# Reordering the end of an attention kernel's load phase: one chunk of q loaded ahead of the last rows of k, k's inverse norms ended on VectorE, and the first tile of v loaded and turned in two halves

## The chip, the cores and the metric

The kernel runs on one core of a Trainium2 chip, as one program. Its time is device time in microseconds (us); the median of the runs is what counts.

The engines are named as in the profile: PE is TensorE (matmuls), PEld its weight loads, DVE is VectorE, ACT is ScalarE, POOL is GpSimd, SP is SyncE. Here POOL issues the loads of q, k, v and the weights, and SP issues the stores and the transposing copies of later v tiles.

## The reference

The arrays q, k and v have the shape (4, 6080, 256) and are float32. For each of the four batches b:

```
qn = q / (norm of q over its 6080 rows + 1e-6)      # one norm per column
kn = k / (norm of k over its 6080 rows + 1e-6)
a  = softmax(kn.T @ qn / tau)                       # 256 x 256, tau = 1
x  = v @ a                                          # 6080 x 256
out = (s * relu(x @ w_in)**2 + b_) @ w_out          # w_in 256 x 2048, w_out 2048 x 256
```

So all of q and k of a batch has to be seen before the first row of its output can be made. After that the work on v is a long stream of matmuls.

## The kernel before

**Stages.** Batch 0's Gram matrix (k.T q, 256 x 256, in `s_ps`) and its column norms are computed first, while q and k arrive. The softmax matrix is never applied to v by itself: `first_block` and `folds` multiply it by w_in, giving `wa` (256 x 2048), and the stream then computes `h = wa.T @ vT` (line 790), relu, square and the second matmul, group after group of 512 rows of v (`mm1`, `relu`, `square`, `plain_mm2`, `seven_items`). The Gram matrices of batches 1 to 3 are interleaved into the stream. The change lies wholly in the stage before the stream and in its first matmuls.

**Chunks.** Batch 0's rows go in 13 chunks: chunks 0 to 10 hold 512 rows (4 rows on each of 128 partitions, `jc` = 4), and chunks 11 and 12 share the last 448 rows (2 rows on each of 112 partitions, `jc` = 2). The last three, 10 to 12, are the `late` ones. For every chunk there are Gram matmuls (`mm`, line 173), squares of k and q (`squares`, lines 198 to 206), and sums of the squares. For the early chunks DVE folds the squares into one tile (`fold`, `into_first`, lines 218 and 232). For the late ones the squares go straight into the norm matmuls: line 271 for k (a row of 256 sums spread over all partitions), line 275 for q (one column of sums for each half); chunk 10's k is first halved by an add (line 248).

**Inverse norms.** `inverse` (line 296) makes 1 / (sqrt(n) + 1e-6) in four ACT steps: Ln, Exp(0.5 x), Ln(x + eps), Exp(-x). k has 256 columns per partition, q two. `scale` (line 321) multiplies `s_ps` by k's inverse norms in two halves into `sm_t`. `exps` (line 327) then applies q's inverse norms as the scale of an Exp and gives `eT`. From `eT` come the row sums (line 367), the first products with w_in (lines 372 and 377), the reciprocal of the sums (line 381) and the scaled `wa` (ACT line 348, DVE line 350).

**Order.** `po` keeps instructions in the order in which the program issues them, so each engine's queue is written by hand. DMA loads all go through POOL's queue in program order; each of them waits for the one eight places ahead of it to have landed. Before the change the end of that queue for batch 0 is: k of chunk 10, k of chunks 11 and 12 (one transfer), q of chunk 10, q of chunk 11, q of chunk 12, v tile 0, then w_in in five pieces (256, 256, 512, 512 and 512 columns).

On the other engines the order before is: all of k's squares (chunk 10 and 11 on ACT, 12 on DVE) and k's norm matmuls, k's four ACT steps, then q's squares on DVE, chunk by chunk with the Gram matmuls of the late chunks, then q's four ACT steps, `scale`, the transposes of v tile 0 on PE with one DVE copy (`transpose_v`, lines 496 and 498), one `keep_busy` matmul (line 583, whose result nothing uses), and `first_block`.

Of the kernel before, what the change touches and what calls it, by code (L numbers as in the profile page):

```python
# [8 lines left out]
FP16 = mybir.dt.float16  # L9
# [7 lines left out]
def kernel(  # L17
# [12 lines left out]
    nc = tc.nc  # L30
    P = 128
# [23 lines left out]
    def po(ins):  # L55

        tc.keep_in_program_order(ins)
        return ins
# [53 lines left out]
    class Gram:  # L112
# [69 lines left out]
        def norm_ops(self, c):  # L182

            qc, kc = self.tiles[c]
            _, np_, jc = self.chunks[c]
            st = {}

            at_end = self.b == 0 and c >= len(self.chunks) - NLATE

            def squares(a, js):  # L190
                def f():
                    if "sq" not in st:
                        if at_end:
                            st["sq"] = late_pool.tile([P, 2, jc, C], FP16, tag=f"sq{c}", name="sq")
                        else:
                            st["sq"] = sq_pool.tile([P, 2, JC, C], FP16, tag="sq", name="sq")
                    if a == 1 and at_end and c == len(self.chunks) - 1:
                        po(nc.vector.tensor_mul(
                            st["sq"][:np_, 1, js, :], kc[:np_, js, :], kc[:np_, js, :]))
                    elif a == 0 and (self.b > 0 or at_end or c % 2 == 0):  # L200
                        po(nc.vector.tensor_mul(  # L201
                            st["sq"][:np_, 0, js, :], qc[:np_, js, :], qc[:np_, js, :]))
                    else:
                        po(nc.scalar.activation(  # L204
                            out=st["sq"][:np_, a, js, :], in_=(qc, kc)[a][:np_, js, :],
                            func=AF.Square))
                return f

            def fold(half, arrays, last):
                def f():  # L210
                    src = st["f", 2 * half] if 2 * half < jc else st["sq"]
                    if ("f", half) not in st:
                        if last:
                            t = f3_pool.tile([P, 2, 1, C], FP16, tag="f3", name="f3")
                        else:
                            t = sq_pool.tile([P, 2, half, C], FP16, tag=f"f{half}", name="f")
                        st["f", half] = t
                    po(nc.vector.tensor_add(  # L218
                        st["f", half][:np_, arrays], src[:np_, arrays, :half, :],
                        src[:np_, arrays, half : 2 * half, :]))  # L220
                    if last and c == 0:
                        self.first = st["f", half]
                    if last and c == 0:
                        for rows in self.rows:
                            rows.append((st["f", half], np_, 1))
                return f

            def into_first():

                dst, src = self.first[:np_], st["f", 1][:np_]  # L230
                if self.b == 0:
                    po(nc.vector.tensor_add(dst, dst, src))  # L232
                else:
                    po(nc.gpsimd.dma_start(out=dst, in_=src, accum_op=ALU.add))  # L234

            def unfolded(a):
                self.rows[a].append((st["sq"], np_, jc))

            ops = []
            for h in range(0, jc, 4):  # L240
                js = slice(h, min(h + 4, jc))
                ops += [squares(1, js), squares(0, js)]
            if at_end:
                def rows(a):
                    if a == 0 or jc == 2:
                        return unfolded(a)
                    half = sq_pool.tile([P, 2, 2, C], FP16, tag="f2", name="half")
                    po(nc.vector.tensor_add(half[:np_, 1], st["sq"][:np_, 1, :2], st["sq"][:np_, 1, 2:]))
                    self.rows[1].append((half, np_, 2))
                return ops + [rows]  # L250
            if jc == 8:
                ops += [fold(4, slice(0, 1), False), fold(4, slice(1, 2), False)]
            ops += [fold(2, slice(0, 2), False), fold(1, slice(0, 2), True)]
            return ops + [into_first] if c > 0 else ops
# [24 lines left out]
        def finish_ops(self):  # L279
# [3 lines left out]
            def inverse(a=None):  # L283

                n = C + CH if a is None else (CH, C)[a]

                def part(i):
                    if i == 0:
                        st["r", a] = sm_pool.tile([P, n], FP32, tag=f"r{a}", name=f"r{a}")
                        if a is None:  # L290
                            st["r", 1], st["r", 0] = st["r", a][:, :C], st["r", a][:, C:]
                    r = st["r", a]
                    func, kw = [(AF.Ln, dict(bias=tiny)), (AF.Exp, dict(scale=0.5)),
                                (AF.Ln, dict(bias=eps)), (AF.Exp, dict(scale=-1.0))][i]
                    sums = self.n_all if a is None else self.n_ps[a]
                    po(nc.scalar.activation(out=r, in_=r if i else sums, func=func, **kw))  # L296
                    if i == 3 and a != 1 and inv_tau != 1.0:
                        po(nc.vector.tensor_scalar_mul(
                            out=st["r", 0], in0=st["r", 0], scalar1=inv_tau))

                return [lambda i=i: part(i) for i in range(4)]
# [57 lines left out]
            def first_block(n):  # L359
# [15 lines left out]
                for m in range(CH):  # L375
                    for j in range(CH):
                        po(nc.tensor.matmul(second[:, m], st["e"][:, j, ts(m, P)],
                                            w_in16[:, j, ds(n, n)], start=(m == 0 and j == 0),
                                            stop=(j == CH - 1), skip_group_check=True))
                st["rs"] = sm_pool.tile([P, CH], FP32, tag="rs", name="rs")  # L380
                po(nc.vector.reciprocal(out=st["rs"], in_=r_ps))
                for f0 in range(0, n, P):
                    for m in range(CH):
                        scaled(f0, P, m, two[m][:, ds(f0, P)])
                for m in range(CH):
                    scaled(n, n, m, second[:, m])

# [88 lines left out]
    def group(g):  # L476
        t0 = g * TG
        return t0, min(TG, NT - t0) // P

    v_tiles, vT_tiles = {}, {}  # L480

    def load_v(g):
        t0, nj = group(g)
        v16 = vpool.tile([P, TG // P, C], FP16, tag="v16", name="v16")
        po(nc.gpsimd.dma_start(  # L485
            out=v16[:, :nj, :],
            in_=v_flat[t0 : t0 + nj * P, :].rearrange("(p j) c -> p j c", j=nj)))
        v_tiles[g] = v16

    def transpose_v(g):  # L490
        _, nj = group(g)
        v16 = v_tiles.pop(g)
        vT_ps = ps_o.tile([P, CH, TG], FP16, tag="o_ps", name="vT_ps")
        for j in range(nj):
            for ch in range(CH):
                po(nc.tensor.transpose(vT_ps[:, ch, ts(j, P)], v16[:, j, ts(ch, P)], ident16))
        vT = vtpool.tile([P, CH, TG], FP16, tag="vT", name="vT")
        po(nc.vector.tensor_copy(out=vT[:, :, : nj * P], in_=vT_ps[:, :, : nj * P]))
        vT_tiles[g] = vT

    def crossbar_v(g):

# [39 lines left out]

    for i in range(2):
        g0.load(len(g0.chunks) - NLATE, (i,))
        g0.load_last(i)
    NW = 512
    w_in_rows = moe_w_in.rearrange("(co p) f -> p co f", p=P)
# [2 lines left out]
        cs = slice(0, CH) if co is None else slice(co, co + 1)  # L550
        po(nc.gpsimd.dma_start(out=w_in16[:, cs, f0:f1], in_=w_in_rows[:, cs, f0:f1]))

    load_v(0)
    load_w_in(0, 2 * P)
    load_w_in(2 * P, NW)
    load_w_in(NW, 2 * NW)
    load_w_in(2 * NW, 3 * NW)
    load_w_in(3 * NW, Dff)
    w_out_rows = moe_w_out.rearrange("(fo p) d -> p fo d", p=P)
# [39 lines left out]

    sum_rows = [rows.pop() for rows in g0.rows]  # L600
    ops = {c: g0.norm_ops(c) for c in late}
    for c in late:
        k_squares, _, into_rows = ops[c]
        k_squares()
        into_rows(1)
        g0.add_norms(1)
    last_sum()
    for rows, row in zip(g0.rows, sum_rows):
        rows.append(row)
    for f in (norms_k, *inverse_k):  # L610
        f()
    for c in late:
        ops[c][1]()
        ops[c][2](0)
        if c == NCH0 - 1:
            norms_q()
        for j in range(g0.chunks[c][2]):
            g0.mm(c, j)
        if c < NCH0 - 1:
            g0.add_norms(0)  # L620
    for f in (*inverse_q, scale_s):
        f()
    transpose_v(0)
    keep_busy(1)
    first_block()

# [146 lines left out]
    def mm1(g, m):  # L773
# [4 lines left out]
        i, fh = divmod(m, 2)  # L778
        if fh == 0:
            h_tiles[g, i] = h_tile("h_ps")  # L780
        h_ps = h_tiles[g, i][:, fh, :]
        for b, p0, p1 in segments(g):
            wa = grams[b].wa
# [274 lines left out]
```

## Time and profile before

| what | value |
|---|---|
| median of 3 runs | 713.63 us (713.52 to 713.67) |
| the profiled execution: its own time | 713.68 us |
| its span in the trace | 712.0 us, so 1.7 us lie around it |
| PE busy in the span | 690.0 us, 97% |
| DVE, ACT, POOL busy | 635.0, 548.2, 109.9 us |
| PE busy from 50 us to the end | 659.09 of 662.00 us |
| PE busy in 24.00 to 31.60, and 31.60 to 38.40 | 4.71 of 7.60, and 6.15 of 6.80 us |

Times in the trace count from the start of the span. A timeline row gives the start, the duration, engine, line, operation, destination and sources, shapes and count. An arrow in brackets is the idle time ahead of the row and what ended it. A row with a count above 1 merges neighbours, and its duration runs from the first start to the last end. An operation's duration holds a fixed part that overlaps with the next operation on the same engine.

### The profile page before, as it was taken

To read this page: it belongs to the slowest core of one execution; us is meant where nothing else is said; L and a number is where in the kernel's file an instruction comes from. 1 tells how busy PE (TensorE), PEld (TensorE's weight loads), DVE (VectorE), ACT (ScalarE), POOL (GpSimd) and SP (SyncE) were. 2 spreads that over 40 slices of the span, in tenths; PEclk is the share of its full clock that TensorE was granted. 3 is DMA by queue.
4 is the path that set the end of the run, shared out by engine and by line. 5 is a ranking of instruction groups with operands and counts; after the bars stand their busy time and mean duration, and the time that the engine had idled before them with its cause. 6 is when DMAs were issued, how large, how long until landed. Compare 5 with 4: busy or idle time off the path is not lost.

```text
span 712.0 us, 17517 instructions
## 1 busy us (share of the span) xinstructions
PE 690.0 (97%) x7422; PEld 501.8 (70%) x7422; DVE 635.0 (89%) x906; ACT 548.2 (77%) x599; POOL 109.9 (15%) x184
## 2 busy tenths in 40 slices
PE   3699999999999999999999999999999999999998
PEld 2456777776677777777677777777768777777777
DVE  3889999999988989998999899998998888888886
ACT  5789877787787777778877777777877777777875
POOL 3433132202102132111010222111000000000000
PEclk9999999999999999999999999999999999999999
DMA  9999999756746889465761888737423333321202
GB/s 240 207 253 158 189 170 132 130 93 123 140 103 107 132 142 152 98 96 102 155 127 50 149 143 143 128 76 100 99 64 74 94 71 76 97 61 46 83 31 75
DMA packets 86846, 83.81 MB, mean 118 GB/s; under 512 B 56240, under 2 KB 62432, under 8 KB 86512
## 3 DMA queue, kind: packets, MB, share of 16 engines
q0 software_dynamic: 26000, 43.74, 38.8%
q1 hardware_dynamic: 60336, 37.71, 22.3%
q8 instruction: 58, 0.95, 0.6%
q10 hardware_dynamic: 432, 1.25, 0.4%
q14 instruction: 20, 0.16, 0.1%
HBM read 78.91 MB, written 24.90 MB: 146 GB/s over the span
## 4 chain that ended last, share of the span: by engine, by line
PE 95%; DVE 2%; DMA 1%; ACT 1%; issue 0%; DVEq 0%
PE h_ps L790 46%; PE o_ps L961 40%; PE s_ps L173 4%; DVE f L218 1%; PE wa_ps L421 1%; DMA raw<-in_q_dram 1%; PE o_ps L865 1%; PE o_ps L837 0%; DVE f L232 0%; ACT r L296 0%; PE wa_ps L355 0%; DVE sq L201 0%; ACT sq L204 0%; ACT qk L164 0%; PE n_ps L271 0%
## 5 line engine op out<-in xcount | busy, mean ns | idle before, releaser
L800 ACT ACTIVATE r<-h_ps 128x1024 f16<-128x1024 f32 (+1 forms) x384 | 388.5, 1013 | 144.5 <-PE h_ps L790 140.9
L790 PE MATMUL h_ps<-vT,wa 128*128 128x512 f16 (+7 forms) x1632 | 451.9, 364 | 0.0
L961 PEld LDWEIGHTS <-S 128*128 128x128 f16 x2944 | 198.1, 98 | 84.3
L961 PEld LDWEIGHTS <-g 128*128 128x128 f16 x2208 | 155.0, 98 | 74.0
L813 DVE TENSOR_TENSOR g<-r 128x2048 f16<-128x2048 f16 (+2 forms) x150 | 174.6, 1164 | 10.0 <-ACT r L800 9.5
L961 PE MATMUL o_ps<-T,S 128*128 128x128 f16 x2208 | 183.1, 219 | 0.0
L790 PEld LDWEIGHTS <-wa 128*128 128x128 f16 x1632 | 136.6, 98 | 18.8 <-ACT wa L348 0.6
L961 PE MATMUL o_ps<-w_out,g 128*128 128x128 f16 x1472 | 134.2, 219 | 0.0
L811 ACT ACTIVATE g<-r 128x1024 f16<-128x1024 f16 (+1 forms) x97 | 100.3, 1034 | 0.2
L818 DVE SCALAR_TENSOR_TENSOR o_sb<-o_ps,s_out,u 128x256 f32<-128x256 f32 x138 | 66.3, 481 | 36.0 <-PE o_ps L961 34.2
L173 PE MATMUL s_ps<-qk 128*128 128x256 f16 (+1 forms) x384 | 68.9, 280 | 16.6 <-ACT qk L164 11.0
L485 POOL DMA_DIRECT2D v<-in_v_dram x48 | 31.4, 662 | 241.0 <-DMA vT<-v 164.5
L234 POOL DMA_DIRECT2D f<-f x33 | 28.9, 875 | 246.9 <-DVE f L218 167.3
L818 DVE SCALAR_TENSOR_TENSOR u<-o_ps,s_out,rowconst 128x256 f32<-128x256 f32 x138 | 65.9, 477 | 0.0
L961 PE MATMUL o_ps<-w_out,S 128*128 128x128 f16 x736 | 63.5, 219 | 0.0
L961 PE MATMUL o_ps<-N,g 128*128 128x128 f16 x736 | 63.4, 219 | 0.0
L890 DVE TENSOR_TENSOR S<-S,g 128x2048 f16<-128x2048 f16 (+1 forms) x47 | 56.4, 1201 | 1.2
L204 ACT ACTIVATE sq<-qk 128x1024 f16<-128x1024 f16 (+2 forms) x53 | 54.5, 1041 | 2.7 <-DVE f L218 2.3
L888 DVE TENSOR_TENSOR S<-g 128x2048 f16<-128x2048 f16 (+1 forms) x47 | 56.1, 1193 | 0.0
L892 DVE TENSOR_TENSOR S<-g 128x2048 f16<-128x2048 f16 x46 | 55.9, 1215 | 0.0
L894 DVE TENSOR_TENSOR S<-g,S 128x2048 f16<-128x2048 f16 x46 | 55.9, 1215 | 0.0
L173 PEld LDWEIGHTS <-qk 128*128 128x128 f16 (+1 forms) x384 | 32.1, 100 | 20.8 <-ACT qk L164 11.0
(109 smaller groups left out, 329.8 us busy)
## 6 DMA issues: line engine op xcount, KB each, us to landing
out_dram<-o_sb SPq DMA_DIRECT2D x41, 512.0 KB, 2.9
v<-in_v_dram POOLq DMA_DIRECT2D x47, 256.0 KB, 4.8
qk<-in_k_dram POOLq DMA_DIRECT2D x36, 256.0 KB, 6.1
qk<-in_q_dram POOLq DMA_DIRECT2D x36, 256.0 KB, 7.1
f<-f POOLq DMA_DIRECT2D x30, 128.0 KB, 3.2
out_dram<-o_sb SPq DMA_DIRECT2D x12, 256.0 KB, 3.9
vT<-v SPq DMA_TRANSPOSE x182, 3.1
w<-in_moe_w_out_dram POOLq DMA_DIRECT2D x4, 512.0 KB, 9.8
```

The costliest lines, as they stand in the source:

```text
L173: po(nc.tensor.matmul(self.s_ps[:, ch, :], qc[:np_, j, ts(ch, P)], kc[:np_, j, :], start=(c == 0 and j == 0 and ch == 0), stop=(c == len(s ...
L204: po(nc.scalar.activation(out=st["sq"][:np_, a, js, :], in_=(qc, kc)[a][:np_, js, :], func=AF.Square))
L790: po(nc.tensor.matmul(dst, wa[:, ci, ts(m, P)], src, start=(ci == 0), stop=(ci == CH - 1), skip_group_check=True))
L800: po(nc.scalar.activation(out=r16[:, :, i % 2, :n], in_=h_tiles.pop((g, i))[:, :, :n], func=AF.Relu))
L811: po(nc.scalar.activation(out=dst, in_=src, func=AF.Square))
L813: po(nc.vector.tensor_mul(dst, src, src))
L818: po(nc.vector.scalar_tensor_tensor(out=dst, in0=src, scalar=s_out, op0=ALU.mult, in1=add, op1=ALU.add))
L888: po(nc.vector.tensor_add(T[1], A21, A22))
L890: po(nc.vector.tensor_sub(T[2], T[1], A11))
L892: po(nc.vector.tensor_sub(T[3], A11, A21))
L894: po(nc.vector.tensor_sub(T[4], A12, T[2]))
L961: po(nc.tensor.matmul(st[name][:, j, :], a()[:, i, ts(j, P)], w[:, i, :], start=first, stop=last, skip_group_check=True))
```

## The change

It has four parts.

1. **Loads.** q of chunk 10 is issued ahead of the transfer with k of chunks 11 and 12. v tile 0 is issued as two halves (2 of its 4 row groups each), the second behind the first two pieces of w_in; w_in's third piece becomes two pieces of 256 columns.
2. **Squares.** ACT squares both k and q of chunk 10; DVE squares both k and q of chunks 11 and 12. Gram matmuls and norm matmuls of the late chunks are put into a new order on PE.
3. **k's inverse norms.** The first two steps, Ln and Exp(0.5 x), stay on ACT. The last two become an add of 1e-6 and a reciprocal on DVE (128 x 256, float32). q's four steps stay on ACT and follow k's two directly.
4. **v tile 0.** Its first half is transposed and copied where the whole was. The second half's four transposes go behind the matmuls of line 377, and their copy into DVE's queue behind the first two scaled pieces of `wa`. The first `h` tile is computed as two halves of 256 columns, for both of its 128-row blocks, so 8 matmuls in place of 4 of 512 columns.

The diff, cut to its core:

```diff
-                    if a == 1 and at_end and c == len(self.chunks) - 1:
...
+                    src = (qc, kc)[a][:np_, js, :]
+                    if jc == 2 or a == 0 and not at_end and (self.b > 0 or c % 2 == 0):
+                        po(nc.vector.tensor_mul(st["sq"][:np_, a, js, :], src, src))
                     else:
                         po(nc.scalar.activation(
+                            out=st["sq"][:np_, a, js, :], in_=src, func=AF.Square))
...
+                    if a == 1 and i == 2:
+                        return po(nc.vector.tensor_scalar_add(out=r, in0=r, scalar1=EPS))
+                    if a == 1 and i == 3:
+                        return po(nc.vector.reciprocal(out=r, in_=r))
...
+                copy = turn_v(0, range(2, 4))
+                del v_tiles[0]
                 st["rs"] = sm_pool.tile([P, CH], FP32, tag="rs", name="rs")
                 po(nc.vector.reciprocal(out=st["rs"], in_=r_ps))
                 for f0 in range(0, n, P):
                     for m in range(CH):
                         scaled(f0, P, m, two[m][:, ds(f0, P)])
+                copy()
...
     for i in range(2):
         g0.load(len(g0.chunks) - NLATE, (i,))
+    for i in range(2):
         g0.load_last(i)
...
-    load_v(0)
+    load_v(0, 0)
     load_w_in(0, 2 * P)
     load_w_in(2 * P, NW)
-    load_w_in(NW, 2 * NW)
+    load_v(0, 1)
+    load_w_in(NW, NW + 2 * P)
+    load_w_in(NW + 2 * P, 2 * NW)
...
+    ops[c0][0]()
+    ops[c0][1]()
+    for j in range(JC):
+        g0.mm(c0, j)
+    add_rows(1, c0)
     last_sum()
+    g0.rows[1].append(sum_rows[1])
+    ops[c1][0]()
+    ops[c2][0]()
+    g0.add_norms(1)
+    add_rows(0, c0)
+    add_rows(1, c1)
+    g0.mm(c1, 0)
+    ops[c2][2](1)
+    for f in (norms_k, *inverse_k[:2]):
         f()
+    ops[c1][1]()
+    g0.mm(c1, 1)
+    g0.rows[0].append(sum_rows[0])
+    add_rows(0, c1)
+    ops[c2][1]()
+    g0.mm(c2, 0)
+    ops[c2][2](0)
+    norms_q()
+    g0.mm(c2, 1)
+    for f in (*inverse_k[2:], *inverse_q, scale_s):
         f()
-    transpose_v(0)
+    turn_v(0, range(2))()
     keep_busy(1)
     first_block()
...
+        if g == 0 and i == 0:
+            for half in range(2 * fh):
+                cols = ts(half, TG // 2)
+                for f in range(2):
+                    for ci in range(CH):
+                        po(nc.tensor.matmul(h_tiles[g, i][:, f, cols], g0.wa[:, ci, ts(f, P)],
+                                            vT[:, ci, cols], start=(ci == 0),
+                                            stop=(ci == CH - 1), skip_group_check=True))
+            return
```

More of the change, by code (lines that the diff above doesn't have):

```diff
@@ L196, in f @@
                             st["sq"] = sq_pool.tile([P, 2, JC, C], FP16, tag="sq", name="sq")
-                    if a == 1 and at_end and c == len(self.chunks) - 1:
[L198 to L202, printed above, removed]
+                    src = (qc, kc)[a][:np_, js, :]
+                    if jc == 2 or a == 0 and not at_end and (self.b > 0 or c % 2 == 0):
+                        po(nc.vector.tensor_mul(st["sq"][:np_, a, js, :], src, src))
                     else:
                         po(nc.scalar.activation(
-                            out=st["sq"][:np_, a, js, :], in_=(qc, kc)[a][:np_, js, :],
-                            func=AF.Square))
+                            out=st["sq"][:np_, a, js, :], in_=src, func=AF.Square))
                 return f
@@ L480, with load_v, turn_v, transpose_v @@
     v_tiles, vT_tiles = {}, {}
-    def load_v(g):
+    def load_v(g, part=None):
         t0, nj = group(g)
-        v16 = vpool.tile([P, TG // P, C], FP16, tag="v16", name="v16")
+        js = slice(0, nj) if part is None else ts(part, 2)
+        if g not in v_tiles:
+            v_tiles[g] = vpool.tile([P, TG // P, C], FP16, tag="v16", name="v16")
         po(nc.gpsimd.dma_start(
[L486 to L492, printed above, removed]
+            out=v_tiles[g][:, js, :],
+            in_=v_flat[t0 : t0 + nj * P, :].rearrange("(p j) c -> p j c", j=nj)[:, js]))
+    def turn_v(g, js):
+        v16 = v_tiles[g]
+        if g not in vT_tiles:
+            vT_tiles[g] = vtpool.tile([P, CH, TG], FP16, tag="vT", name="vT")
         vT_ps = ps_o.tile([P, CH, TG], FP16, tag="o_ps", name="vT_ps")
-        for j in range(nj):
+        for j in js:
             for ch in range(CH):
                 po(nc.tensor.transpose(vT_ps[:, ch, ts(j, P)], v16[:, j, ts(ch, P)], ident16))
-        vT = vtpool.tile([P, CH, TG], FP16, tag="vT", name="vT")
-        po(nc.vector.tensor_copy(out=vT[:, :, : nj * P], in_=vT_ps[:, :, : nj * P]))
-        vT_tiles[g] = vT
+        cols = ds(js[0] * P, len(js) * P)
+        return lambda: po(nc.vector.tensor_copy(out=vT_tiles[g][:, :, cols],
+                                                in_=vT_ps[:, :, cols]))
+    def transpose_v(g):
+        turn_v(g, range(group(g)[1]))()
+        del v_tiles[g]
     def crossbar_v(g):
@@ L601, with add_rows @@
     ops = {c: g0.norm_ops(c) for c in late}
[L602 to L606, printed above, removed]
-    last_sum()
-    for rows, row in zip(g0.rows, sum_rows):
-        rows.append(row)
-    for f in (norms_k, *inverse_k):
-        f()
[L612 to L621, printed above, removed]
+    c0, c1, c2 = late
+    def add_rows(a, c):
+        ops[c][2](a)
+        g0.add_norms(a)
+    ops[c0][0]()
[3 more added lines that the diff above has]
+    add_rows(1, c0)
+    last_sum()
+    g0.rows[1].append(sum_rows[1])
[7 more added lines that the diff above has]
+    for f in (norms_k, *inverse_k[:2]):
+        f()
+    ops[c1][1]()
[8 more added lines that the diff above has]
+    for f in (*inverse_k[2:], *inverse_q, scale_s):
         f()
-    transpose_v(0)
+    turn_v(0, range(2))()
     keep_busy(1)
```

## The prediction

> **What bounds the kernel now.** I read the page's chain first, then the chain in order of time for 26 to 50 us, the timelines of ACT, DVE and PE over the same stretch, and the DMA issues. By the page the chain is PE almost throughout:
>
> ```profile
> PE 95%; DVE 2%; DMA 1%; ACT 1%; issue 0%; DVEq 0%
> ```
>
> From 37.4 us to the end it is matmul after matmul, so a shift of the stream's start goes through to the end one for one. The change touches only what comes before that. There the chain in order of time reads:
>
> ```profile
> 31.64 0.95 PE n_ps L271 x7
> ...
> 32.61 0.48 ACT r L296
> ...
> 33.12 0.43 ACT r L296
> ...
> 33.57 0.52 ACT r L296
> ...
> 34.11 0.58 ACT r L296 x2
> ...
> 35.27 0.21 ACT r L296
> ...
> 35.51 0.52 ACT eT L327
> ...
> 36.91 0.45 PE wa_ps L377 x4
> ...
> 37.40 1.04 PE h_ps L790 x4
> ```
>
> k's norm sums end at 32.6; ACT then runs k's four steps and, queued behind them, q's four; the first Exp of the softmax (eT) starts at 35.51, which I call T. The stream starts at T + 1.89. DVE's view shows what else was ready by then:
>
> ```profile
> 31.50 0.42 DVE L198 TENSOR_TENSOR sq<-qk 112x512 f16<-112x512 f16 x1
> 31.84 0.41 DVE L232 TENSOR_TENSOR f<-f,f 128x512 f16<-128x512 f16 x1
> 32.17 1.35 DVE L201 TENSOR_TENSOR sq<-qk 128x1024 f16<-128x1024 f16 x3
> 34.88 0.76 DVE L321 TENSOR_TENSOR sm_t<-s_ps,r 128x256 f32<-128x256 f32 x2 [1.35 <-PE s_ps L173]
> 35.55 0.68 DVE L498 COPY vT<-vT_ps 128x1024 f16<-128x1024 f16 x1
> ```
>
> The first half of sm_t is ready at 35.30, 0.2 us ahead of q's last step (35.27 + 0.20). DVE has 1.35 us free before it.
>
> **1. The loads.** Landing is issue plus the time to landing:
>
> ```profile
> qk<-in_k_dram POOLq DMA_DIRECT2D x1, 224.0 KB, 11.8
> ...
> qk<-in_q_dram POOLq DMA_DIRECT2D x1, 256.0 KB, 10.8
> ```
>
> Issued at 18.83 and 20.99, they land at 30.6 and 31.8; k of chunk 10 lands at 29.5 (17.20 + 12.3), q of chunks 11 and 12 at 32.3 and 32.9. DMA is busy throughout, 256 KB taking 1.2 us. So the swap gives q of chunk 10 at 30.7 and k's last rows at 31.8; q's last rows stay at 32.9, since the bytes ahead of them are the same. On POOL's queue two issues are added (0.55 to 0.75 us each); they stand behind all of q and k. The pieces that matter later have slack: w_in's first two landed at 34.9 and 35.6 for uses at 36.14 and 36.75, now earlier by half a v tile (0.6 us); v's second half lands near 35.6 and is needed after T + 1.6. Cost nothing, covered by these margins.
>
> **2. Squares and sums of k.** DVE: chunk 10's halving at 31.17, the last fold at 31.50, k's squares of chunk 11 at 31.84 (rows at 31.8) and chunk 12 at 32.17, ending 32.59; then q's at 32.51 and 32.93 (rows at 32.9), ending 33.35. In place of ACT's 0.63 us for k of chunk 11, ACT squares q of chunk 10, 30.7 to 31.8, idle there before. PE: chunk 10's Gram matmuls move into its idle time of 1.84 us ahead of 31.64; k's sums of chunk 11 (2 matmuls, 0.11 each) go at 32.3, two Gram matmuls behind them, and the sums of chunk 12 from 32.75, ending at 33.13 (the last lasts 0.27). So k's Ln starts at 33.16 and not at 32.61: +0.55, because k's last rows come 1.2 us later, part of it taken back by the DVE order.
>
> **3. k's inverse norms.** ACT: Ln 33.16, Exp 33.67 (spacing 0.51 as now), ending 34.09. q's Ln follows 0.32 behind the start of k's last Exp, as now (34.11 to 34.43), so at 33.99, with q's sums in by 33.9. From q's Ln to eT it was 34.43 to 35.51, 1.08. The q side would allow T = 35.07, 0.44 earlier. The k side now goes through DVE: add at 34.12, reciprocal, sm_t (0.42), eT 0.03 later.
>
> The add: float32 tensor-tensor operations on 128 x 256 take 0.42 here (lines 635, 653); if a single-source form on float32 ran at the two elements in 1.04 ns that line 498's copy shows on f16 (1024 in 0.68), it would be 256 x 1.04 / 2 ns + 0.15 = 0.28. I take 0.42, the measured row; the reciprocal starts at 34.58 (a dependent DVE operation starts 0.035 after the end of its source, as between two lines 218).
>
> The reciprocal is the large unknown. The trace has only ones of 2 elements:
>
> ```profile
> 163.56 0.16 DVE L342 RECIPROCAL rs<-r_ps 128x2 f32<-128x2 f32 x1
> 163.63 0.20 DVE L402 TENSOR_TENSOR S<-eT 128x128 f16<-128x128 f16 x1
> ```
>
> Ordinary DVE operations cost 1.04 ns an element (421 ns at 256 float32 in line 321, 684 at 512 in line 308) plus 0.15 fixed in duration, or plus 0.067 from start to start (line 308 to its successor: 600 ns for 512). The reciprocal lasts 157 to 161 ns, 7 to 11 over the fixed part, and its successor starts 77 ns after it, 10 over: for two elements, 3.5 to 5.5 ns each. I take 5 ns, which both readings allow: 256 x 5 + 150 = 1.43 us. Lower end: the excess is a longer pipeline and an element costs 1.04 ns, 0.42 us. Upper end: the fixed part is 144, as in the 145 ns of the one-element tensor-scalar of line 699, and the highest reading, 161, gives 8.5 ns: 2.33 us.
>
> [...]
>
> Sum: 34.58 + 1.43 = 36.01; sm_t 36.04 to 36.46; T = 36.49, against 35.51: **+0.98 us**. The two ACT steps removed (1.0 us) and the earlier q side are covered by the k side. Nothing else queues behind the reciprocal but sm_t and the copy of v's first half, which has until T + 1.9.
>
> **4. v in halves.** The first four transposes and their copy lie in idle time, as the eight did. The other four come between line 377 and line 790. There PE has issued its last matmul of line 377 at 37.08 and could go on at 37.19, but starts line 790 at 37.40, waiting for wa. Four at 0.056 fill 0.22 of 0.21: no cost. The copy costs: DVE's second scaled piece starts at T + 1.76 and frees the queue 0.27 later; the transposes are through at T + 2.06; the copy runs T + 2.09 to T + 2.51 (0.42 at 128x512). The first half of h (4 x 0.108) is done issuing at T + 2.34; the second waits for the copy and issues T + 2.54 to T + 2.97. Before, the four wide matmuls were issued by 38.27, T + 2.76. **+0.2 us**, bounds 0 (copy ready in time) and 0.35. DVE's third scaled piece, waiting on the copy now, ends near T + 3.05, ahead of its use at T + 3.2. Behind that the matmuls follow one another as before.
>
> **Total** 0.98 + 0.2 = +1.18 on a profiled execution of 713.68 (span 712.0), so a span near 713.2; on the median, 713.63 + 1.18 = **714.8**. A change within 0.2% (1.43 us) is about what a measurement of this kernel can tell from no change: the forecast is slightly slower, inside that band.
>
> **Rivals.**
>
> *The reciprocal is cheap* (1.04 ns an element). T = 34.58 + 0.42 + 0.03 + 0.42 + 0.03 = 35.48, and +0.2: 713.8; with the add at 0.28, 713.6. Were DVE no limit at all, the q side gives T = 35.07: -0.44 + 0.2, 713.4. The reading of 7 to 11 ns speaks against it, but it rests on two elements. No branch reaches 712.2, as q's last rows still land at 32.9.
>
> *The reciprocal is slow* (7 to 8.5 ns). At 8: 256 x 8 + 150 = 2.20, T = 37.26, total +1.95: 715.6, slower. It decides from 6 ns on: 1.43 - 0.2 - 0.98 = 0.25 us over 256 elements is 1.0 ns above my 5. The small operation's reading speaks against, the fixed part's uncertainty for it.
>
> *PE's clock falls in the longer wait.* PE would idle from the end of the idle matmul near 34.8 to T + 0.56 = 37.05, 2.2 us. If it slowed: the first 18 Gram matmuls at 11 us came 0.213 apart, later ones 0.109, so 18 x 0.104 = +1.9, 716.7. Against: PE idled 2.8 us ahead of 23.27 and went on at full rate.
>
> **How the numbers follow.** Forecast 0.5 (a quarter of it past 1.43, since 6 ns lie within its reach), cheap 0.26, slow 0.2, clock 0.03, something unseen on the gain side 0.01. Slower by over 0.2%: 0.12 + 0.2 + 0.03 = 0.35; faster 0.02 (with a little for the unseen); within 0.63. The range 713.4 to 715.9 takes in the cheap branch to its floor and the slow one at 8 and a little more; it leaves out the clock and the ends.
>
> **What the profile after would show.** k's Ln near 33.2; a RECIPROCAL of 128x256 of 1.2 to 1.7 us, ending near 36.0; eT released by DVE's sm_t near 36.5 and not by ACT; line 381's reciprocal 1.2 behind eT; the first h matmuls in two fours with a gap of 0.2. Wrong if the reciprocal lasts under 0.6 or over 2, if eT is released by ACT, if PE's spacing behind T is above 0.11, or if PE shows new waits after 45 us.

## The result: slower by 0.4%, outside the forecast's range

| | median of 6 runs, us | lowest to highest |
|---|---|---|
| before | 713.66 | 713.52 to 715.21 |
| after | 716.75 | 715.59 to 717.58 |

The ratio after / before is 1.0038 [1.0025, 1.0051], +3.1 us; the forecast was 714.8 (713.4 to 715.9). The mean clock granted to TensorE (PE) is 0.993 to 0.997 of full speed in the six runs after and 0.995 to 0.998 in 78 of the 107 runs of before that lie beside the versions below, and the runs of one kernel lie up to 2 us apart. The profiled execution after took 716.02 (span 714.3, before 712.0).

The page's chain after, against PE 95%, DVE 2% before, is still PE nearly throughout:

```profile
PE 96%; DMA 3%; DVE 1%; POOL 0%; issue 0%; ACT 0%; POOLq 0%; DVEq 0%
```

The chain in order of time after (start, duration, what) shows what now stands where the eight ACT steps stood between k's norm sums and eT:

```profile
33.58 0.48 ACT r L296
...
34.54 0.30 DVE r L290
...
34.87 1.76 DVE r L292
...
36.72 0.76 DVE sm_t L321 x2
...
38.65 0.45 PE wa_ps L377 x4
...
39.14 0.61 DVE wa L350 x2
...
40.13 0.60 PE h_ps L810 x4
```

k's Ln starts at 33.58 (predicted 33.16, before 32.61), the reciprocal lasts 1.75 us (predicted 1.43), and T, the start of the first softmax Exp, is 37.24 (predicted 36.49, before 35.51). By the same chain h's first tile is through, and PE goes on to line 355, at T + 3.49 (40.73); before it was at T + 2.93 (38.44). So 1.73 us are lost up to T and 0.56 behind it, 2.29 of the span's 2.3. From there the two streams are the same. PE's timeline shows two things that the forecast had ruled out (start, duration, count, idle time ahead and its releaser). First the kernel before, then after:

```profile
23.27 1.05 PE L173 MATMUL s_ps<-qk 128*128 128x256 f16 x8 [2.83 <-DMA qk<-in_q_dram]
```

```profile
23.46 1.89 PE L173 MATMUL s_ps<-qk 128*128 128x256 f16 x8 [2.82 <-DMA qk<-in_q_dram]
...
25.58 1.93 PE L173 MATMUL s_ps<-qk 128*128 128x256 f16 x8
...
34.49 0.47 PE L595 MATMUL idle_ps<-fill 128*128 128x512 f32 x1
37.81 0.20 PE L367 MATMUL r_ps<-parts,eT 128*128 128x1 f16 x2 [2.85 <-DVE vT L503]
...
38.49 0.60 PE L377 MATMUL wa_ps<-w_in,eT 128*128 128x256 f16 x4
```

The same wait for the same load, 2.8 us long, is followed by eight matmuls in 1.05 us in one execution and by eight in 1.89 in the other: whether PE keeps its clock behind such a wait is not decided by its length alone. In this execution the granted clock is 0.50, half speed, from 22.67 to 29.49, for 6.82 us, and 1.00 from 30 us to the end; k's Ln, at 33.58, starts 0.42 later than in the version with the wait filled, below (33.16). And ahead of eT, PE now idles 2.85 us where it idled 0.57. Behind that wait this execution has the full clock (line 377's four matmuls in 0.60 us). It took 716.02, and four of the other five 716.72 or more, so what most of them lose is not in this trace; the experiments have to show it.

### The profile page after: what moved, and what is told of

It reads as the page before. It is cut to its first block, busy times and chain, and to the rows that moved or that the text cites. A ratio compares the mean times of both kernels' runs of the same rounds, so it can differ in the third digit from the quotient of the medians.

```text
span 714.3 us, 17528 instructions
## 1 busy us (share of the span) xinstructions
PE 693.0 (97%) x7426; PEld 503.8 (71%) x7426; DVE 636.9 (89%) x909; ACT 547.8 (77%) x597; POOL 111.3 (16%) x186
## 4 chain that ended last, share of the span: by engine, by line
PE 96%; DMA 3%; DVE 1%; POOL 0%; issue 0%; ACT 0%; POOLq 0%; DVEq 0%
PE h_ps L823 46%; PE o_ps L994 40%; PE s_ps L173 5%; DMA qk<-in_q_dram 3%; PE wa_ps L424 1%; PE o_ps L898 1%; PE o_ps L870 0%; POOL qk L142 0%; PE wa_ps L355 0%; PE idle_ps L595 0%; DVE r L292 0%; PE n_ps L267 0%; ACT r L296 0%; DVE sm_t L321 0%; DVE vT L503 0%
## 5 line engine op out<-in xcount | busy, mean ns | idle before, releaser
L173 PE MATMUL s_ps<-qk 128*128 128x256 f16 (+1 forms) x384 | 72.1, 290 | 15.4 <-ACT qk L164 11.2
L201 ACT ACTIVATE sq<-qk 128x1024 f16<-128x1024 f16 (+1 forms) x53 | 55.0, 1049 | 2.8 <-DVE f L214 2.3
```

Of the source, the lines that this page charges most:

```text
L173: po(nc.tensor.matmul(self.s_ps[:, ch, :], qc[:np_, j, ts(ch, P)], kc[:np_, j, :], start=(c == 0 and j == 0 and ch == 0), stop=(c == len(s ...
L201: po(nc.scalar.activation(out=st["sq"][:np_, a, js, :], in_=src, func=AF.Square))
```

## The experiments

Each version was run 5 to 11 times in turn with the kernel before; the lines shown are of its one profiled execution, and their line numbers, of the version's own file, differ by a few from one version to the next. The kernel before stood at 713.61 to 713.66 on all the chips used.

**Which wait costs the clock?** Theory A: the longer wait ahead of eT leaves PE idle, and the half-speed stretch falls on the first matmuls of the stream in nearly every run. Theory B: it is the early stretch, ahead of 23.5 us, which delays k's sums. Four kernels tell these apart and price k's steps on VectorE (DVE).

*k's steps back on ScalarE (ACT)*, all else as after:

```diff
-                    if a == 1 and i == 2:
-                        return po(nc.vector.tensor_scalar_add(out=r, in0=r, scalar1=EPS))
-                    if a == 1 and i == 3:
-                        return po(nc.vector.reciprocal(out=r, in_=r))
```

> The kernel after, with k's last two steps as Ln and Exp on ScalarE again; all else as after. Clock by the wait (theory A: the long wait for the reciprocal leaves PE idle, and that halves PE's clock): T falls by 0.76 us (k's four steps 1.92 us from 33.58, then q's 1.08 behind its Ln, T = 36.48 in place of 37.24) and the wait is shorter, so the clock returns to 1.00 and the time to 715.0 or less. Clock by the early gap (theory B: PE's idle time ahead of 23.4 us, in code that the change does not touch): clock still 0.995, 716.0. Clock harmless (theory C: the half-speed stretch lies in PE's idle time and costs nothing): 716.0, whatever the clock.

Measured: 715.77 (714.38 to 716.13), ratio 1.0023 [1.0015, 1.0032]. T is 36.04, but PE idles 2.08 us ahead of eT, and behind that wait line 373's four matmuls, 0.60 at full speed, take 1.06 us; line 351's, from 40.30 on, take 0.60 again, and h's first tile is through at T + 4.4. Theory A had expected the clock back and 715.0 or less here, as the wait is shorter; in this execution half speed follows 2.08 us all the same. The runs show both cases side by side: eight of the eleven, with a mean granted clock of 0.995, took 715.75 to 716.13, and the three at 1.00 took 714.38, 714.67 and 715.09. So even without the reciprocal the changed order loses the clock in most runs.

*The wait filled*, after with nine idle matmuls:

```diff
-    keep_busy(1)
+    keep_busy(9)
     first_block()
```

> The kernel after, with 9 idle matmuls in place of 1 between the transposes of v's first half and the first matmul on eT, 2.1 us of PE's wait of 3.2 us. A: clock 1.00, 715.0 to 715.5. B: the early gap is untouched, clock 0.995 and 716.7 as after. C: no change of time.

Measured: 715.49 (715.30 to 715.77), ratio 1.0024 [1.0015, 1.0033]: 1.26 us better than after, and a narrow spread. In its profiled execution a half-speed stretch still lies early, at 23.8 to 27.2 (granted clock 0.62 in 23 to 26.5, 0.90 in 26.5 to 30), but k's sums are not late, and from 30 to 46 us the clock is 1.00. Over its eleven runs that stretch costs nothing that can be seen: the three at a mean clock of 1.00 took 715.51 to 715.77. So its ACT and DVE timelines are the undisturbed picture of the change:

```profile
33.16 0.47 ACT L296 ACTIVATE r<-n_ps,tiny 128x256 f32<-128x256 f32 x1 [1.39 <-PE n_ps L267]
```

```profile
34.12 0.29 DVE L290 TENSOR_SCALAR r<-r 128x256 f32<-128x256 f32 x1 [0.74 <-ACT r L296]
34.44 1.75 DVE L292 RECIPROCAL r<-r 128x256 f32<-128x256 f32 x1
36.30 0.76 DVE L321 TENSOR_TENSOR sm_t<-s_ps,r 128x256 f32<-128x256 f32 x2
```

k's Ln is at 33.16, to the hundredth where the prediction put it; T is 36.82, +1.31; h's first tile is through at T + 3.46.

*The early wait filled*, after with ten idle matmuls ahead of 23 us:

```diff
-    FILL = {-8: 1, -7: 1, -6: 1, -5: 2, -4: 2}
+    FILL = {-8: 10, -7: 1, -6: 1, -5: 2, -4: 2}
```

> The kernel after, with 10 idle matmuls in place of 1 behind chunk 5 (2.4 us of PE's idle time between 20.6 and 23.5 us). A: the clock is lost in the wait all the same, no change of time. B: clock 1.00, 715.0 to 715.8. C: clock 1.00 and no change of time beyond the 0.23 us by which k's Ln came late, so 716.5.

Measured: 716.85 (716.15 to 717.55), ratio 1.0040 [1.0027, 1.0052]: nothing gained. The windows view gives, per stretch, its length, each engine's busy time, and PE's granted clock as the column ahead of the last two. With the early wait filled, for 36 to 39 and 39 to 42.5 us:

```profile
36.00:39.00 3.00, 1.64 (x12) 1.11 (x13) 1.67 (x6) 1.53 (x4) 2.94 (x5) 0.51 1.26 200
39.00:42.50 3.50, 3.50 (x19) 2.48 (x18) 1.74 (x6) 1.44 (x2) 1.62 (x3) 0.50 1.06 328
```

T is 36.80, as in the version with the late wait filled, but the clock is halved straight through the start of the stream, where that version has 1.00, and its matmuls are stretched accordingly, so that h's first tile is through at T + 4.70 in place of T + 3.46. Line 377 with the early wait filled, and then with the late wait filled:

```profile
38.30 1.06 PE L377 MATMUL wa_ps<-w_in,eT 128*128 128x256 f16 x4
```

```profile
38.06 0.60 PE L377 MATMUL wa_ps<-w_in,eT 128*128 128x256 f16 x4
```

The 1.24 us between them are of the size of the 1.26 above; they are not the same quantity, as this execution is one of the long ones (717.55) and its stretch goes on to 42.9 (granted clock 0.94 in 42.5 to 46). Theory B falls; A stands.

*k's two last steps alone on DVE*, in the kernel before:

```diff
+                    if a == 1 and i == 2:
+                        return po(nc.vector.tensor_scalar_add(out=r, in0=r, scalar1=EPS))
+                    if a == 1 and i == 3:
+                        return po(nc.vector.reciprocal(out=r, in_=r))
...
-    for f in (norms_k, *inverse_k):
+    for f in (norms_k, *inverse_k[:2]):
...
-    for f in (*inverse_q, scale_s):
+    for f in (*inverse_k[2:], *inverse_q, scale_s):
```

> The kernel before, with only k's last two inverse-norm steps moved to VectorE (add 0.29, reciprocal 1.75): Ln k 32.61 as before, Exp to 33.54, add to 33.86, reciprocal to 35.64, sm_t to 36.12, T = 36.15 in place of 35.51, so +0.64 and no other cost: 714.3. A: as the wait is 0.64 longer, the clock may fall and the time rise to 715 or more. B and C: 714.3, clock as before.

Measured: 714.75 (714.30 to 716.18), ratio 1.0012 [1.0003, 1.0021]; T is 36.39 (+0.88). The expected 714.3 was too low by 0.45: T came 0.24 later than expected, of which k's Ln, at 32.73, is 0.12, and h's first tile is through 0.18 later behind T (T + 3.11), which is taken up below. PE idles 1.33 us ahead of eT here, and behind it line 381's four matmuls take 0.60 us, as at full speed; ten of the eleven runs lie at 714.30 to 715.02, one at 716.18.

**Half of the fill.** Would a shorter gap do?

```diff
-    keep_busy(1)
+    keep_busy(4)
     first_block()
```

> The changed kernel with four idle matmuls in the wait where it has one and the filled version has nine (716.7 and 715.5). An idle matmul takes 0.28 us, so TensorE's idle time ahead of eT goes from 2.85 us to 2.0. If any gap under 2.9 us is harmless, 715.5; if the clock goes by how much of a stretch of some 3.4 us is idle, and not by one unbroken gap, a part of the runs stays near 716.7 and the median lies between.

Measured: 716.72 (715.60 to 717.03), ratio 1.0039 [1.0027, 1.0052], no better than after. In PE's timeline the gap ahead of eT is 2.06 us, and line 355's four matmuls, 0.60 at full speed, take 1.06:

```profile
37.48 0.20 PE L367 MATMUL r_ps<-parts,eT 128*128 128x1 f16 x2 [2.06 <-DVE vT L503]
...
40.68 1.06 PE L355 MATMUL wa_ps<-w_in,eT 128*128 128x256 f16 x4
```

Four runs of five lie where those of after lie (716.7 to 717.0), one does not (715.60). By their times, then, the clock is lost with a gap of 2.06 us in four runs of five, and with nine idle matmuls (gap 0.61) in none of eleven. The version with k's steps alone lies between: with its gap of 1.33 us one run of eleven is long. Gaps between 1.33 and 2.06 were not tried, and what rule sets it, no run shows.

**The first 0.4 us behind T.** In after, in the filled version and in the one with k's steps alone, DVE's first scaled piece of wa (line 350) starts at T + 1.87 to T + 1.90 and not at T + 1.49, although its inputs are ready as early (rs and line 372's products at T + 1.37 and T + 1.40 in the last, T + 1.37 and T + 1.41 in the kernel before). All three have two more DVE instructions ahead of it. Theory P: its place in DVE's instruction stream decides. Theory V: the reciprocal or the order around it does. Two dummies, in the kernel before and in the filled version:

```diff
+    for n in range(2):
+        nc.vector.memset(consts.tile([P, 1], FP32, name=f"spare{n}"), 1.0)
```

> The kernel before with two more memsets of 128x1 on VectorE among the constants, which nothing reads; nothing else is changed. It asks why VectorE starts its first scaled piece of wa about 0.4 us late in the changed kernel, in the version with the wait filled and in the one with only k's reciprocal on VectorE, all of which put two more instructions on VectorE ahead of it. Theory P (the place in VectorE's instruction stream decides): the first scaled piece starts near T + 1.9 instead of T + 1.49, T being the start of the first softmax Exp, and the median goes from 713.6 to about 714.0. Theory V (the long reciprocal or the order around it does it): T + 1.49 as before, 713.6.

> The changed kernel with nine idle matmuls in the wait (715.49 on the chip of the other runs, first scaled piece at T + 1.87) and the same two memsets. Theory P: the first scaled piece goes back to T + 1.5, the second half of h comes 0.2 to 0.4 sooner, 715.1 to 715.3. Theory V: T + 1.87 and 715.5 as without them.

Measured: the kernel before with dummies 714.07 (713.75 to 715.39), ratio 1.0012 [1.0003, 1.0020]; the filled version with dummies 715.25 (715.11 to 715.50), ratio 1.0024 [1.0014, 1.0033], 0.24 better than without. DVE's timelines, of before, of before with the dummies (T = 35.44), and of the filled version with them (T = 36.77):

```profile
36.71 0.17 DVE L381 RECIPROCAL rs<-r_ps 128x2 f32<-128x2 f32 x1 [0.48 <-PE r_ps L367]
37.00 0.61 DVE L350 TENSOR_SCALAR wa<-wa_ps,rs 128x128 f16<-128x128 f32 x2
```

```profile
36.64 0.17 DVE L381 RECIPROCAL rs<-r_ps 128x2 f32<-128x2 f32 x1 [0.48 <-PE r_ps L367]
37.33 1.08 DVE L350 TENSOR_SCALAR wa<-wa_ps,rs 128x128 f16<-128x128 f32 x3 [0.52 <-PE wa_ps L377]
```

```profile
38.25 0.61 DVE L350 TENSOR_SCALAR wa<-wa_ps,rs 128x128 f16<-128x128 f32 x2
38.87 0.43 DVE L503 COPY vT<-vT_ps 128x512 f16<-128x512 f16 x1
```

From the reciprocal's start to the first piece it is 0.29 us in the first and 0.69 in the second: two memsets that touch nothing make the delay, and in the changed kernel two more take it away (T + 1.48, 0.28 behind the reciprocal). Theory P holds in both directions. It moves h's first tile from T + 2.93 to T + 3.11 in the kernel before, and from T + 3.46 to T + 3.18 in the filled version. The page's "PE wa_ps L377" is only the last event before the start; line 377's end is not what is waited for: with the early wait filled its four matmuls run from 38.30 to 39.36, and the late piece starts at 38.77. The other versions fit: where DVE has two more instructions ahead of that piece it starts 0.67 to 0.69 us behind the reciprocal's start, and where it has none or four more, 0.28 to 0.29; only the version with k's steps on ACT and no filled wait lies between, with 0.44, at half clock. Why the place matters, no run shows. Among the runs of before with dummies five of eleven lie at 715.1 to 715.4, against three of the 32 of before beside them; why the two memsets should raise that share stays open, and so the +0.4 of that median is not the price of the delay alone (its six other runs lie at 713.75 to 714.07).

**v's halves.** The filled version with v whole, and the filled version without k's steps on DVE (with six idle matmuls), once with v whole and once with the halves. The edit for v whole, cut to its core; the second half's transposes and copy and the split of h's first tile go too:

```diff
-    load_v(0, 0)
+    load_v(0)
...
-    load_v(0, 1)
-    load_w_in(NW, NW + 2 * P)
-    load_w_in(NW + 2 * P, 2 * NW)
+    load_w_in(NW, 2 * NW)
...
-    turn_v(0, range(2))()
+    transpose_v(0)
```

> The changed kernel with nine idle matmuls in the wait and v's first tile loaded, turned and used whole, as in the kernel before; the loads' order and k's two steps on VectorE stay. If the halves are what puts h's first tile at T + 3.46 where it was at T + 2.93, it comes back to T + 2.95 and the median is 713.6 + 1.3 = 714.9. If VectorE's late start does it, it stays near T + 3.3 and the median near 715.3. By my prediction's sum for the halves (0.2), 715.3 with T + 3.25.

> The first part of the change alone, with the order of the late steps around it: q's four rows loaded ahead of k's last, k's four steps on ScalarE, v whole, and six idle matmuls in the wait so that TensorE's clock is no matter. k's Ln at 33.15 as predicted, T near 36.0 (+0.5), h's first tile at T + 2.93, so 714.1 if the shift of k's rows is paid in full; 713.6 if q's earlier rows give it back.

> The changed kernel with k's four steps on ScalarE and six idle matmuls in the wait, v's halves included: against the same version with v whole (714.25) it prices the halves alone, with VectorE's instructions at the places they have in the kernel before. My prediction's sum for them was 0.2: 714.45. If the halves cost nothing but for the place of VectorE's instructions, 714.25; if they cost 0.4, 714.65.

Measured: with k's steps on DVE and v whole 715.08 (714.91 to 715.31), 1.0021 [1.0013, 1.0030]; k's steps on ACT, v whole 714.25 (713.85 to 714.52), 1.0006 [0.9997, 1.0015]; k's steps on ACT, v in halves 714.42 (714.27 to 714.53), 1.0010 [1.0001, 1.0019]. The first is 0.41 below its twin with halves, but it still has DVE's late start (h's first tile at T + 3.12), and in its trace T is 0.27 earlier as well (36.55), for a reason that no run isolates, so it does not price the halves by itself. The last two have DVE's pieces at their old place, and do: 714.42 - 714.25 = +0.17 (+0.20 if each is taken against the kernel before beside it); by their chains h's first tile is at T + 3.18 and T + 2.92, 0.26 apart. The reordered loads alone stand at +0.59, with T at 36.03.

**Is there a version that gains?** If k's inverse norms are what makes the earlier q rows worthless, fewer steps should release them. Ln and Exp(-0.5 x) give 1/sqrt(n) in two steps; three kernels use them for the first batch, whose lines are shown here, and one fills the idle stretches of the kernel before:

```diff
+                    if a is not None:
+                        func, kw = [(AF.Ln, dict(bias=tiny)), (AF.Exp, dict(scale=-0.5))][i]
+                    else:
...
```

> The kernel before with two steps in place of four for the first item's inverse norms, Ln and Exp(-0.5 x), and two idle matmuls in the wait; it leaves out the 1e-6 that the reference adds to the norms (of about 7.8). k's two last steps leave ScalarE with nothing in their place. T is then bound by the Gram matmuls' end (34.8), near 35.25 (-0.25), so 713.4.

> The changed kernel's order of loads and late steps (q's four rows ahead of k's last), v whole, and two steps for the inverse norms as in the version of before, without the 1e-6. Where k's inverse norms no longer bound T, the earlier q rows should count: the Gram matmuls end near 34.0 in place of 34.8, T near 34.6 (-0.9), so 712.8. If the earlier q rows are worth nothing, T near 35.2 and 713.4.

> The whole changed kernel, v's halves included, with two steps on ScalarE (Ln, Exp(-0.5 x)) for the first item's inverse norms and nothing of them on VectorE; it leaves out the 1e-6 that the reference adds to the norms. The version with v whole stood at 713.13 with T at 34.53; its wait was w_in's second block, for which line 377's matmuls stood idle 0.57 us. The halves put that block ahead of v's second half. If that is what they are worth, line 377 no longer waits, T stays near 34.5 and the median is 712.6 to 712.8; if the halves cost 0.2 to 0.4 whatever T is, 713.3 to 713.5.

```diff
-    FILL = {-8: 1, -7: 1, -6: 1, -5: 2, -4: 2}
+    FILL = {-8: 8, -7: 1, -6: 1, -5: 4, -4: 6}
...
-    keep_busy(1)
+    keep_busy(3)
```

> The kernel before with TensorE's idle stretches ahead of the softmax filled: 8, 4, 6 and 3 idle matmuls where it has 1, 2, 2 and 1. The kernel before has its half-speed stretch in places where it does little harm, and at 715.0 to 715.2 in some 12% of its runs. If those runs are the clock's, they go, and the rest stays at 713.5 to 713.7; if not, some 12% stay at 715.

Measured: two steps in the kernel before 713.54 (713.35 to 714.97), ratio 1.0000 [0.9992, 1.0009], T = 35.19; two steps in the changed order with v whole 713.13 (712.99 to 713.29), 0.9991 [0.9982, 1.0000], T = 34.53; the same with v in halves 713.58 (713.20 to 714.57), 1.0000 [0.9991, 1.0009], T = 34.51; the filled kernel before 713.86 (713.76 to 714.09), 1.0001 [0.9992, 1.0010].

T comes forward by 0.98 us in all: 0.32 by the two steps alone (35.19), and 0.66 by the order of the change on top (34.53), as soon as k's inverse norms do not bind. Half of it is then lost to the next wait, the load of w_in's second block: the median falls by 0.51, not by the 0.8 expected. PE with v whole, and then with v in halves:

```profile
36.50 0.60 PE L376 MATMUL wa_ps<-w_in,eT 128*128 128x256 f16 x4 [0.57 <-DMA w_in<-in_moe_w_in_dram]
```

```profile
35.75 0.60 PE L376 MATMUL wa_ps<-w_in,eT 128*128 128x256 f16 x4
36.47 0.40 PE L500 MATMUL vT_ps<-ident,v 128*128 128x128 f16 x4
...
68.83 0.39 PE L173 MATMUL s_ps<-qk 128*128 128x256 f16 x2 [0.24 <-DMA qk<-in_q_dram]
```

The halves do what they are for: line 376 no longer waits. But the transposes of v's second half start only at 36.47, as their weight loads wait 0.40 us for v's second half to land, and line 354's matmuls behind h's first tile start at 37.82, against 37.80 with v whole. In its profiled execution a wait at 68.8, for rows of the second batch, puts it a further 0.4 behind the other, which does not have it; whether it is there in every run is open. So the 712.6 to 712.8 that the halves might have given did not come, and the version with v whole is the fastest of all: each of its eleven runs is under each of the 27 runs of before beside it (lowest 713.35), by 0.5 us in the medians, 0.07%, though the 95% interval of the ratio ends at 1.0000, and with the 1e-6 left out of the norms. The filled kernel before shows the granted clock 1.00 in all eleven runs and none near 715. The kernel before itself, over the 107 runs beside the versions, agrees: of the 29 with a mean clock of 0.999 or 1.00 none lies above 714.0, and of the 78 below that twelve lie at 714.7 to 715.2. So the long runs of before go with the clock, though most runs with a lost clock are not long. But in the filled version q's last squares wait for their load until 33.91, as they do (33.76) in the other version with the early wait filled; T is later (35.78), and it gains nothing.

## Why the prediction was wrong, by its own steps

The medians give the bill. Each row is the difference of two versions that differ in that part. In the first and the third the number of idle matmuls in the wait differs too, and in the third the two dummies, which keep DVE's first piece on time:

| step of the prediction | predicted | measured | from |
|---|---|---|---|
| 1 and 2, loads and k's sums | +0.55 | +0.59 | 714.25 - 713.66 |
| 4, v in halves | +0.2 | +0.17 | 714.42 - 714.25 |
| 3, k's two steps on DVE | +0.43 | +0.83 | 715.25 - 714.42 |
| DVE's first piece delayed by its place | none | +0.24 | 715.49 - 715.25 |
| PE's clock in the wait | 0 (rival, 0.03) | +1.26 | 716.75 - 715.49 |
| sum | +1.18 | +3.09 | |

**The step that failed is the dismissal of the clock.** The prediction computed the longer wait, named the rival, and set it aside with one row: PE idled 2.8 us ahead of 23.27 and went on at full rate. One row of one execution could not carry that. In the execution after the same gap was followed by half speed, and in the traces of the versions that lost the clock at the stream the gap was 2.06 to 2.12 us. What the kernel before had was not an immunity. In the trace of before with the two dummies a slow stretch lies between 24 and 28 us (two groups of eight Gram matmuls in 1.70 and 1.89 us, the next, at 28.37, in 1.05), where PE still waits for loads, and k's Ln, at 32.55 (before 32.61), is not late; behind the wait ahead of eT, 0.56 there and 0.57 in before, both traces have the clock at 1.00 (36 to 42.5 us). The signs that the prediction named would not have shown this in the profile after: the reciprocal is under 2 us, eT waits for DVE, and PE's spacing behind T is 0.11, as in this execution the half-speed stretch ends at 29.49. The rival's 716.7 came near the median, but partly by luck: it charged 1.9 us for a stretch that cost 1.26, and lacked the other misses. Without the clock the change stands at 715.49, inside the range of the forecast, though not within 0.2%, where its likeliest case lay.

**The reciprocal was mis-sized.** It lasted 1.75 us, (1.75 - 0.15) / 256 = 6.25 ns an element with the prediction's fixed 0.15, not the 5 read from the two-element rows: +0.32. That is past the 6 ns from which the rival "slow" was said to decide, and short of its 7 to 8.5. The add took 0.29, the lower of the two readings and not the 0.42 taken: -0.13. sm_t and eT started later behind their sources than counted, by 0.14 together. Together T is 0.33 later than 36.49 in the undisturbed trace (36.82).

**Behind T, the plan was right, the start was not.** With DVE's first piece on time the trace follows the prediction: the copy of v's second half runs from T + 2.10, 0.43 long (predicted T + 2.09 to T + 2.51), and the halves cost 0.17. What was not foreseen, and stood in no term of the sum, is that two more instructions on DVE move the first piece by 0.4.

**What was right.** The loads cost nothing by themselves; k's Ln at 33.16; eT released by DVE's sm_t and not by ACT; q's earlier rows covered by the k side. The statement that the q side would allow an earlier T was tested by the two-step version: T = 34.53, below even the 35.07 computed, as there q's Ln starts at 33.86 and q has two steps, which end at 34.33.

## What to carry to other kernels

A wait that is lengthened on the path can cost twice if PE idles in it, as the gaps of 2.06 us and more did here in most runs: once for itself and once for the clock behind it (0.83 and 1.26 us in this change). Before such a change is made, don't trust one gap in one execution that went well; fill the wait with idle matmuls, so that the two costs can be told apart, and look at the clock of every run. And bringing data earlier is worth something only where the next step is not already waiting for another chain; here the same reordering cost 0.6 us with four steps for k's norms, and gained 0.4 us with two (713.13 against 713.54).

## What the runs showed of the hardware that was not expected

- A float32 RECIPROCAL of 128x256 on VectorE takes 1.75 us, 6 times the 0.29 of the add of a constant to the same tile.
- With waits of 2.06 to 2.82 us on PE, half speed comes in some executions, for some 3.4 us (39.0 to 42.5 with half of the fill, where the wait ends at 37.48) or 6.82 us (22.67 to 29.49 after, where it ends at 23.46), and not in others (eight matmuls in 1.05 us behind 2.83 us in the kernel before). With nine idle matmuls (2.70 us of work) in the wait the clock is 1.00 from 30 to 46 us; with four it is 0.51 from 39 to 42.5.
- Two memsets of 128x1 that nothing reads, run 35 us earlier, delay a later VectorE instruction by 0.4 us; two more, in a kernel that has the delay, remove it.
